# Low half of a weight pair by one VectorE subtraction in place of a cast and an adding DMA, with a newly planned order, in a chain of attention and two expert layers

## The chip, the cores and the metric

The kernel runs on one core of a Trainium2 chip. The metric is the time of one execution in microseconds (us) on the device, the median over several runs. Inputs and outputs lie in HBM.

## The reference

The reference chains three blocks on 1536 rows of 512 numbers (float32). Local attention with a window of 16 keys on each side, plus 24 block summaries for each head, gives `x`. Then come two layers of dense experts, 4 experts in the first and 8 in the second:

```
for e in range(E):                      # E = 4, then 8
    h = np.maximum(x @ w1[e], 0.0)      # 512 -> 1024
    out += p[:, e:e + 1] * (h @ w2[e])  # 1024 -> 512
```

In the first layer `p` are the given shares of each row, divided by their sum. In the second, `p` comes from a gate, `x @ w_gate`, and eight rounds in which rows and columns are normalised in turn.

## The kernel before

**Units and steps.** A unit is one expert's slice of 256 hidden columns: 16 units in the first layer, 32 in the second, so 48 in all. A step is one unit on one of the two halves of 768 rows (`b` = 0 or 1), so there are 96 steps. Each step has a first part (`add_first`, tensors `w1`, matmuls at L294) and a second part (`add_second`, tensors `w2`, matmuls at L593). The second part of a step runs interleaved with the first part of the next step.

**Seven products.** Both parts multiply 2 x 2 blocks by a scheme of seven products instead of eight, so weights and rows enter as blocks and as sums of blocks. The operands of the weights are named A11, A12, A22, S1, S2, S3 and S4, where the S are sums. The orders in which a step does its products are written out by hand as strings (`FIRST`, `SECOND`), in which digit 5 is the product with S1, 6 the one with S2, 3 with S4 and 7 with S3.

**High and low halves.** Every operand is held as two float32r tensors, a rounded high half and a low half that holds the rest. A product is three matmuls of 128 x 384 in a row: high by high, high by low, low by high. The tiles are `w1hi`, `w1lo`, `w2hi`, `w2lo` for weights, `xhi`, `xlo`, `x11..` for the rows of the first part and `hoph` for both halves of the rows of the second.

**Weights** (`add_weights`). SyncE loads the four blocks of a slice into a raw buffer (three of these turn: `raw1`, `raw2` and `xf`). ScalarE casts three blocks to the high half (L471) and writes the same blocks, negated and rounded, to the low half (L472); GpSimd then starts a DMA that adds the raw blocks to the low half (L475), so that the rest stays there. Then three adding DMAs in place (L482) make the sums in the raw buffer. Then the pair S1, S2 and the pair S4, S3 get the same treatment as the blocks: cast, negated write, adding DMA, each 128 x 512. Blocks A12, A22, A11 have two sets of slots that alternate by unit. The four sums have only one set, so the cast of a new pair waits until TensorE has read the old pair for the last time.

**Row operands.** `add_hop` prepares the operands of the second part: ScalarE writes the high half (L453), VectorE the low half by one subtraction (`lo_op`, L448 or L443). Results are added up by VectorE (L229) or by ScalarE copies through PSUM (L604).

**Who sets the order.** All work is collected with `op(engine, span, reads, writes, due, ...)` and put in order by `run_work`, a planner that runs when the program is built. It knows a time for each kind of work (`SPAN`; for DMAs four numbers: issue, start-up, time on the shared DMA engines, landing), takes the work that can start first by those times, and breaks ties by `due`, which is counted in steps. The instructions then stand in each engine's queue in that order, and each queue is executed in order. `LEAD` and `LEAD2` say how many steps ahead weights and their pairs are due, `HOP` and `DCOFF` when the operands and the second half of the columns of the second part are due, `ALONG`, `FIRST0`, `XDUE`, `W0DUE`, `XPOOL` place the attention, the first step, the row operands and the first weights, `TURN`, `LATER` and `SOONER` place work around the border between the layers (`add_turn`, `add_scale`).

Of the kernel before, what the change touches and what calls it, by code (L numbers as in the profile page):

```python
# [18 lines left out]
def local_global_attention_moe_moe(  # L19
# [287 lines left out]
    def relu(S, out, src, th, neg=False):  # L307
# [9 lines left out]

    ADD = 0.72  # L320
    SPAN = {
# [5 lines left out]
        "v1536": (1.3, 1.34), "vmax": (0.57, 0.65), "vsum": (0.57, 0.66), "vrec": (0.12, 0.18),  # L327
        "vks": (0.6, 0.69), "vks2": (0.35, 0.42), "vkw": (0.7, 0.81), "vq": (1.0, 1.1),
        "vvb": (0.22, 0.3), "vmk": (0.82, 0.83), "vid": (1.1, 1.15),
        "a": (0.41, 0.48), "ah": (0.42, 0.52), "a512": (0.53, 0.63), "a768": (0.74, 0.84),  # L330
        "as": (0.2, 0.26), "akw": (0.8, 0.91), "aq": (0.95, 1.04), "aexp": (1.05, 1.12),
        "ax": (0.31, 0.38),
        "p256": (0.75, 0.77), "p384": (1.05, 1.08), "psm": (0.98, 1.02), "pks": (0.8, 0.85),
        "pid": (0.55, 0.6), "p1": (0.2, 0.25), "pmask": (3.0, 3.1), "psel": (0.9, 0.95),
        "add1": (0.87, 1.2, ADD, 1.2), "add2": (0.87, 1.2, 2 * ADD, 1.2),
        "add3": (0.87, 1.2, 3 * ADD, 1.2), "ld": (0.45, 1.0, 0.6, 1.8), "st": (0.45, 0.5, 0.5, 1.2),
        "ldk": (0.45, 1.0, 0.8, 1.2), "ldv": (0.45, 1.0, 1.3, 1.2), "lds": (1.4, 1.6, 1.2, 1.2),
        "ldp": (0.45, 1.0, 0.5, 1.2),
    }
    HOP_WAIT = 0.09  # L340
    work = []
    last_write, last_reads = {}, {}

# [92 lines left out]
    def aop(fn, reads, writes, due, span="a", use=None):  # L436
        op("ACT", span, reads, writes, due, fn, use=use)
# [17 lines left out]
    def add_weights(u, kind, start):  # L455
        hi, lo = wop[kind]
        i = turn_of(kind, u)
        R = [("raw", i, j) for j in range(4)]
        for o, x, blocks in loads(kind, u):
            first = XF if (kind, u) == (1, 2) else []  # L460
            op(
                "SP", "ld", [("mark", WAIT0)] if u == 0 else (),
                [R[j] for j in blocks] + first, start,
                lambda o=o, x=x: nc.sync.dma_start(out=o, in_=x),
            )

        def group(s, src, blocks, key, due, span):
            n = len(blocks)
            h, l = hi[:, s:s + n], lo[:, s:s + n]
            rd = [R[j] for j in blocks]  # L470
            aop(lambda: nc.scalar.copy(out=h, in_=src), rd, [key + ("hi",)], due, span)  # L471
            aop(lambda: nc.scalar.mul(l, src, -1.0), rd, [key + ("lo",)], due, span)  # L472
            op(
                "POOL", f"add{n}", rd, [key + ("lo",)], due + 0.05,
                lambda: nc.gpsimd.dma_start(out=l, in_=src, accum_op=ALU.add),  # L475
            )

        group(slot(u, A12), raws[i][:, 0:3], (0, 1, 2), wkey(kind, u, A12), start + 0.2, "a768")
        for o, x, wr, rd in sums_of(kind, u):
            op(  # L480
                "POOL", f"add{len(wr)}", [R[j] for j in (*rd, *wr)], [R[j] for j in wr], start + 0.5,
                lambda o=o, x=x: nc.gpsimd.dma_start(out=o, in_=x, accum_op=ALU.add),  # L482
            )
        group(6, *pair_of(kind, u, 0), wkey(kind, u, S1), start + LEAD2, "a512")
        group(8, *pair_of(kind, u, 1), wkey(kind, u, S4), start + LEAD2 + 0.1, "a512")

    def wk(kind, u, x):
        k = wkey(kind, u, x)
        return [k + ("hi",), k + ("lo",)]
# [505 lines left out]
    def add_loads(i, d):  # L995
        b, hp = pairs[i]
        for j in range(2):
            op(
                "SP", "ldk", (), [("kn", j)] + ([("mark", i)] if j else []), d,
                lambda j=j: nc.sync.dma_start(  # L1000
                    out=kn[:, :, j, :], in_=k[b, 2 * hp + j].rearrange("(c p) d -> p c d", p=P)
                ),
            )
        for j in range(2):
            op(
                "SP", "ldk", (), [("qn", j)], d + 0.01,
                lambda j=j: nc.sync.dma_start(
                    out=qn[:, j],
                    in_=q[b, 2 * hp + j].rearrange("(c p r) d -> p c (r d)", p=P, r=2),
                ),  # L1010
            )
        op(
            "SP", "ldv", (), ["vn"], d + 0.3,
            lambda: nc.sync.dma_start(
                out=vn, in_=v[b, 2 * hp:2 * hp + 2].rearrange("h (p c) d -> p h c d", c=VC)
            ),
        )
        t = vs[i % 2]

        def windows(j):  # L1020
            src = v[b, 2 * hp + j]
            mid = bass.AP(
                src.tensor, src.offset + (QT - WIN) * D, [[D, KW], [QT * D, NQ - 2], [1, D]]
            )
            nc.sync.dma_start(out=t[0:KW, 0, j, :], in_=src[0:KW, :])
            nc.sync.dma_start(out=t[0:KW, 1:NQ - 1, j, :], in_=mid)
            nc.sync.dma_start(out=t[0:KW, NQ - 1, j, :], in_=src[S - KW:S, :])

        for j in range(2):
            op("SP", "lds", (), [("vs", i % 2, j)], d + 0.35, lambda j=j: windows(j))  # L1030

    def add_keys(i, d):
# [50 lines left out]
        def spread():  # L1083
# [4 lines left out]
                )  # L1088

        op(  # L1090
            "POOL" if KSPOOL else "DVE", "pks" if KSPOOL else "vks",
            [("ks", p, 0), ("ks", p, 1)], [("kw", p, 2)], d + 0.03, spread,
        )

# [152 lines left out]
    def add_rows_first(d):  # L1247
        op(
            "SP", "ldp", [("mark", 1)], ["dp"], d,
            lambda: nc.sync.dma_start(out=dp, in_=domain_probs.rearrange("(t p) e -> p t e", p=P)),  # L1250
        )
        op(
            "SP", "ldp", [("mark", 1)], ["wg"], d,
            lambda: nc.sync.dma_start(out=wg, in_=w_gate.rearrange("(c p) e -> p c e", p=P)),
        )

        def shares():
            nc.vector.tensor_reduce(out=dsum, in_=dp, axis=AX.X, op=ALU.add)
            nc.vector.tensor_scalar_add(out=dsum, in0=dsum, scalar1=1e-9)
            nc.vector.reciprocal(out=dsum, in_=dsum)  # L1260
            nc.vector.tensor_tensor(
                out=p1.rearrange("x e t -> x t e"), in0=dp,
                in1=dsum[:, :, None].to_broadcast([P, NTT, E1]), op=ALU.mult,
            )

        vop(shares, ["dp"], ["p1"], d, "v768", True)
        tk = take_of(0)
        n = E1 * NTT
        op(
            "PE", "tr", ["p1", "ident"], ["prt"], d,  # L1270
            lambda: nc.tensor.transpose(
                full[tk["bank"]][0:n, 0:P], p1.rearrange("x e t -> x (e t)"), ident
            ),
            take=tk,
        )
        aop(
            lambda: nc.scalar.copy(out=rowt[0:n], in_=full[tk["bank"]][0:n, 0:P]),
            ["prt"], ["rowt"], d, "as", use=tk,
        )
        op("SP", "st", ["rowt"], ["prow1"], d, lambda: save_rows(0))  # L1280

        def halves():
            nc.scalar.copy(out=wghl[:, :, 0:E2], in_=wg)

        def lows():
            nc.vector.tensor_tensor(
                out=wghl[:, :, E2:2 * E2], in0=wg, in1=wghl[:, :, 0:E2].bitcast(F32),
                op=ALU.subtract,
            )
            nc.vector.tensor_tensor(  # L1290
                out=fold, in0=ident[0:2 * E2, 0:E2], in1=ident[0:2 * E2, E2:2 * E2], op=ALU.add
            )

        aop(halves, ["wg"], ["wghi"], d + 4.0, "as")
        vop(lows, ["wghi", "ident"], ["wghl"], d + 4.0, "vs", True)

    def set_places():

# [18 lines left out]
    L = E1 * NFU - 1  # L1317
    steps = [(u, b, 2 * u + b) for u in range(NU) for b in range(2)]
    border = 2 * L + 1
    FIRST = {0: "1567324", 1: "1562374"}  # L1320
    SECOND = {0: "1256437", 1: "1524637"}
    HOP, GOFF, DCOFF, LEAD, LEAD2 = 1.15, 0.16, 3.9, 1.0, 0.97
    LOPOOL = ()
    ALONG = 8.8
    NARROW = 4
    WAIT0 = 2
    KSPOOL = False
    XDUE = [-5.4, -2.8, -2.0, 0.3]
    W0DUE = -3.0
    FIRST0 = -1.1  # L1330
    XPOOL = [(B22, T3), (N1, B21, T3, N4), (T3, N4), (B22, N4)]
    LATER = {1: -0.4, 2: -0.4, 3: 0.6, 8: -0.4}
    SOONER = {0: 0.4, 2: -0.4, 3: -0.4, 6: 0.2, 7: 0.2}
    TURN = 0.8
    M2ACT = True
    with tc.manual_schedule():
        ps = ctx.enter_context(tc.tile_pool(name="ps", bufs=1, space=PSUM))
        full = [ps.tile([P, 512], F32, name=f"bank{i}") for i in range(8)]
# [33 lines left out]
        op("SP", "ld", ["prow1"], [("pb", 1)], -0.5, lambda: load_row(PB[1], 0, 0, 1))  # L1372
        for j, key in enumerate(("pz", ("bank", 3), ("bank", 4), ("bank", 5), ("bank", 6))):
            op(
                "PE", "one", [("x", 0, 0, B11)] + wk(1, 0, A11), [key], 0.1,
                lambda j=j: nc.tensor.matmul(
                    cut[2 + j], wop[1][0][:, SLOT[A11], 0:P], x_of(0, 0, 0, B11),
                    start=True, stop=True, skip_group_check=True,
                ),
            )  # L1380
# [65 lines left out]
```

## Time and profile before

| | |
|---|---|
| median of 3 runs | 1564.73 us (1563.39 to 1567.13) |
| profiled execution, own time | 1563.7 us |
| span from first to last instruction | 1562.0 us |
| TensorE (PE) busy | 1522.5 us, 97% |
| weight loads (PEld) busy | 1489.1 us, 95% |
| VectorE (DVE) busy | 1303.5 us, 83% |
| ScalarE (ACT) busy | 1201.3 us, 77% |
| GpSimd (POOL) busy | 608.7 us, 39% |
| granted TensorE clock, mean | 0.997 of 2.4 GHz |
| DMA started by GpSimd | 151.03 MB, 60.6% of the 16 DMA engines |

The times of engines are unions of their instructions' times, and overlap. A matmul that follows another closely starts before the other's record ends. The profiled execution took 1.0 us less than the median.

### The profile page before, as it was taken

How to read it: one execution, taken by the hardware profiler on the slowest of the kernel's cores; microseconds unless marked ns; L12 is line 12 of the kernel's file. 1: busy time of each engine (PE TensorE's matmuls, PEld its weight loads, DVE VectorE, ACT ScalarE, POOL GpSimd, SP SyncE). 2: the span in 40 equal slices, each digit the busy share in tenths (PEclk: the TensorE clock that was granted, in tenths of full speed). 3: DMA queues.
4: the chain of work that ended last, by engine and by line, in shares of the span. 5: the costliest groups of instructions: out<-in, count | busy, mean ns of one | idle time of the engine just before them, and what ended most of it. 6: DMA issues, size and time to landing. Idle time of an engine off the chain costs nothing.

```text
span 1562.0 us, 26666 instructions
## 1 busy us (share of the span) xinstructions
PE 1522.5 (97%) x9106; PEld 1489.1 (95%) x9106; DVE 1303.5 (83%) x2717; ACT 1201.3 (77%) x2587; POOL 608.7 (39%) x632
## 2 busy tenths in 40 slices
PE   8899999999999999999999999999999999999998
PEld 7799999999999988999999999999999999999997
DVE  7787788788888897899888888888888887888888
ACT  6798688687777779777777778777877877868865
POOL 3553434434343332333343343443434343443430
PEclk9999999999999999999999999999999999999999
DMA  9978888878778874697878778878878887888863
GB/s 213 219 152 148 149 154 149 150 146 153 147 149 149 149 130 94 120 182 133 149 142 156 149 139 161 153 139 155 146 139 159 149 145 150 150 149 150 151 108 95
DMA packets 223865, 231.13 MB, mean 148 GB/s; under 512 B 48736, under 2 KB 169968, under 8 KB 223728
## 3 DMA queue, kind: packets, MB, share of 16 engines
q0 software_dynamic: 107520, 151.03, 60.6%
q1 hardware_dynamic: 116208, 78.39, 17.9%
q8 instruction: 71, 1.16, 0.3%
q14 instruction: 66, 0.54, 0.1%
HBM read 73.97 MB, written 3.22 MB: 49 GB/s over the span
## 4 chain that ended last, share of the span: by engine, by line
PE 72%; DMA 14%; DVE 5%; issue 4%; ACT 3%; POOL 2%; SPq 0%; POOLq 0%; ACTq 0%; DVEq 0%
PE bank L294 34%; PE bank L593 33%; DMA w2lo<-raw 4%; DMA w1lo<-raw 2%; DMA w2lo<-xf 2%; DMA w1lo<-xf 2%; DMA raw<-raw 2%; DVE acc L229 1%; PE bank L1168 1%; DMA vn<-in_v_dram 1%; PE bank L1132 1%; PE bank L1229 1%; ACT hoph L453 1%; PE bank L1214 1%; DVE hoph L448 1%
## 5 line engine op out<-in xcount | busy, mean ns | idle before, releaser
L593 PE MATMUL bank<-hoph,w2hi 128*128 128x384 f32 x2688 | 687.9, 336 | 9.0 <-ACT bank L604 6.1
L593 PEld LDWEIGHTS bank<-hoph,w2hi 128*128 128x128 f32 x2688 | 483.1, 188 | 14.8 <-ACT bank L604 8.3
L593 PE MATMUL bank<-hoph,w2lo 128*128 128x384 f32 x1344 | 451.8, 336 | 8.7 <-DMA w2lo<-raw 6.0
L229 DVE TENSOR_TENSOR acc<-bank,acc 128x384 f32<-128x384 f32 x736 | 392.5, 551 | 7.0 <-PE bank L593 5.0
L294 PE MATMUL bank<-xhi,w1hi 128*128 128x384 f32 x1008 | 339.7, 337 | 1.8 <-ACT xhi L453 1.1
L294 PE MATMUL bank<-xlo,w1hi 128*128 128x384 f32 x1008 | 337.8, 335 | 0.4 <-DVE xlo L443 0.4
L294 PE MATMUL bank<-xhi,w1lo 128*128 128x384 f32 x1008 | 337.6, 335 | 0.2 <-DMA w1lo<-xf 0.2
L482 POOL DMA_DIRECT2D raw<-raw x195 | 194.7, 1000 | 304.3 <-DMA raw<-raw 182.6
L604 ACT COPY bank<-bank 128x384 f32<-128x384 f32 x384 | 181.1, 472 | 153.8 <-PE bank L593 146.8
L453 ACT ACTIVATE hoph<-q 128x384 fp32r<-128x384 f32 x576 | 288.6, 519 | 7.7 <-PE bank L593 4.3
L448 DVE TENSOR_TENSOR hoph<-q,hoph 128x384 fp32r<-128x384 f32 x486 | 259.7, 549 | 27.1 <-ACT hoph L453 26.9
L593 PEld LDWEIGHTS bank<-hoph,w2lo 128*128 128x128 f32 x1344 | 252.2, 188 | 15.2 <-DMA w2lo<-raw 10.6
L294 PEld LDWEIGHTS bank<-xhi,w1hi 128*128 128x128 f32 x1008 | 189.5, 188 | 5.4 <-ACT xhi L453 1.4
L294 PEld LDWEIGHTS bank<-xlo,w1hi 128*128 128x128 f32 x1008 | 189.6, 188 | 0.7 <-DVE xlo L443 0.7
L294 PEld LDWEIGHTS bank<-xhi,w1lo 128*128 128x128 f32 x1008 | 189.5, 188 | 0.5 <-DMA w1lo<-xf 0.5
L475 POOL DMA_DIRECT2D w1lo<-raw x96 | 95.3, 993 | 173.8 <-ACT w1lo L472 136.1
L482 POOL DMA_DIRECT2D xf<-xf x93 | 92.3, 992 | 166.1 <-DMA xf<-xf 101.0
L604 ACT COPY acc<-bank 128x384 f32<-128x384 f32 x220 | 105.0, 479 | 56.3 <-PE bank L593 46.6
L475 POOL DMA_DIRECT2D w2lo<-raw x99 | 108.5, 1098 | 93.4 <-ACT w2lo L472 53.5
L604 ACT COPY bank<-acc 128x384 f32<-128x384 f32 x176 | 85.1, 483 | 55.3 <-DVE acc L229 51.5
L311 DVE SCALAR_TENSOR_TENSOR q<-bank,pb 128x384 f32<-128x384 f32 x180 | 99.5, 553 | 23.2 <-PE bank L294 18.9
L232 DVE TENSOR_TENSOR q<-q,bank 128x384 f32<-128x384 f32 x96 | 53.1, 553 | 71.0 <-PE bank L294 68.1
(180 smaller groups left out, 2168.3 us busy)
## 6 DMA issues: line engine op xcount, KB each, us to landing
raw<-raw POOLq DMA_DIRECT2D x130, 256.0 KB, 3.8
raw<-in_moe_w_dram SPq DMA_DIRECT2D x66, 256.0 KB, 5.0
w2lo<-raw POOLq DMA_DIRECT2D x66, 256.0 KB, 4.1
raw<-in_moe_w_dram SPq DMA_DIRECT2D x128, 128.0 KB, 3.3
w1lo<-raw POOLq DMA_DIRECT2D x64, 256.0 KB, 4.0
xf<-xf POOLq DMA_DIRECT2D x62, 256.0 KB, 3.8
w2lo<-raw POOLq DMA_DIRECT2D x33, 384.0 KB, 5.4
w1lo<-raw POOLq DMA_DIRECT2D x32, 384.0 KB, 5.7
```

Of the source, the lines that this page charges most:

```text
L229: (eng or nc.vector).tensor_tensor(out=out, in0=x, in1=y, op=ALU.add)
L232: (eng or nc.vector).tensor_tensor(out=out, in0=x, in1=y, op=ALU.subtract)
L294: nc.tensor.matmul(pm, l[:, s, cs_], x_of(b, c, r, x), start=first and i == 0, stop=i == n - 1, skip_group_check=True,)
L311: nc.vector.scalar_tensor_tensor(out=out, in0=src, scalar=0.0, in1=PB[S[1]][:, th * HB:(th + 1) * HB], op0=ALU.min if neg else ALU.max, op ...
L448: e.tensor_tensor(out=out, in0=src, in1=hi.bitcast(F32), op=ALU.subtract)
L453: aop(lambda: nc.scalar.mul(to(0), src, -1.0 if neg else 1.0), reads, writes, due, "ah")
L475: lambda: nc.gpsimd.dma_start(out=l, in_=src, accum_op=ALU.add),
L482: lambda o=o, x=x: nc.gpsimd.dma_start(out=o, in_=x, accum_op=ALU.add),
L593: nc.tensor.matmul(cut[bank], l[:, s, cols], hop_of(t, r), start=start and i == 0, stop=i == 2, skip_group_check=True,)
L604: aop(lambda: nc.scalar.copy(out=out, in_=src), [kin], [kout], due)
L1132: nc.tensor.matmul(pv[KW:KX, 0:P], sel[:, c, :], vn[:, :, c, :], start=c == 0, stop=c == VC - 1,)
L1168: nc.tensor.matmul(pw[:, tt * KX:(tt + 1) * KX], bd[p][:, g * GT + tt].rearrange("x j q -> x (j q)"), kw[p][(g * GT + tt) // KT][:, (g * G ...
```

## The change

In `add_weights` the function `group` gets a switch. For the pairs named in `LODVE`, which is the pair S1, S2 of both `w1` and `w2`, the low half is made by one VectorE subtraction, raw minus high half, as `lo_op` does it for rows. ScalarE's negated write and GpSimd's adding DMA of that pair fall away. The pair S4, S3 and the three blocks stay as they were. The planner's times of DMAs and a few names of spans are new, and its constants are new, so the order of all work is planned anew.

```diff
-    ADD = 0.72
+    ADD = 1.0
...
-        "add1": (0.87, 1.2, ADD, 1.2), "add2": (0.87, 1.2, 2 * ADD, 1.2),
-        "add3": (0.87, 1.2, 3 * ADD, 1.2), "ld": (0.45, 1.0, 0.6, 1.8), "st": (0.45, 0.5, 0.5, 1.2),
-        "ldk": (0.45, 1.0, 0.8, 1.2), "ldv": (0.45, 1.0, 1.3, 1.2), "lds": (1.4, 1.6, 1.2, 1.2),
-        "ldp": (0.45, 1.0, 0.5, 1.2),
+        "add1": (0.95, 1.3, ADD, 1.2), "add2": (0.950001, 1.3, 2 * ADD, 1.2),
+        "add3": (0.950002, 1.3, 3 * ADD, 1.2), "ld": (0.45, 1.0, 0.65, 1.3),
+        "st": (0.450001, 0.5, 0.5, 1.2), "ldk": (0.450002, 1.0, 1.2, 1.2),
+        "ldq": (0.450003, 1.0, 0.6, 1.2), "ldv": (0.450004, 1.0, 1.0, 1.2),
+        "lds": (1.4, 1.6, 1.8, 1.2), "ldp": (0.450005, 1.0, 0.6, 1.2),
...
-    HOP_WAIT = 0.09
+    HOP_WAIT = 0.08
...
-        def group(s, src, blocks, key, due, span):
+        def group(s, src, blocks, key, due, span, by_dve=False):
             n = len(blocks)
             h, l = hi[:, s:s + n], lo[:, s:s + n]
             rd = [R[j] for j in blocks]
             aop(lambda: nc.scalar.copy(out=h, in_=src), rd, [key + ("hi",)], due, span)
+            if by_dve:
+                vop(
+                    lambda: vsub(l, src, h.bitcast(F32)), rd + [key + ("hi",)],
+                    [key + ("lo",)], due + 0.05, "v512",
+                )
+                return
             aop(lambda: nc.scalar.mul(l, src, -1.0), rd, [key + ("lo",)], due, span)
...
-        group(6, *pair_of(kind, u, 0), wkey(kind, u, S1), start + LEAD2, "a512")
-        group(8, *pair_of(kind, u, 1), wkey(kind, u, S4), start + LEAD2 + 0.1, "a512")
+        for i, s in enumerate((S1, S4)):
+            group(
+                SLOT[s], *pair_of(kind, u, i), wkey(kind, u, s), start + LEAD2 + i / 10, "a512",
+                (kind, s) in LODVE,
+            )
...
-    FIRST = {0: "1567324", 1: "1562374"}
+    FIRST = {0: "5162374", 1: "1562374"}
     SECOND = {0: "1256437", 1: "1524637"}
-    HOP, GOFF, DCOFF, LEAD, LEAD2 = 1.15, 0.16, 3.9, 1.0, 0.97
+    HOP, GOFF, DCOFF, LEAD, LEAD2 = 1.18, 0.16, 3.1, 1.93, 0.99
     LOPOOL = ()
-    ALONG = 8.8
+    ALONG = 8.2
...
-    XDUE = [-5.4, -2.8, -2.0, 0.3]
-    W0DUE = -3.0
-    FIRST0 = -1.1
-    XPOOL = [(B22, T3), (N1, B21, T3, N4), (T3, N4), (B22, N4)]
-    LATER = {1: -0.4, 2: -0.4, 3: 0.6, 8: -0.4}
-    SOONER = {0: 0.4, 2: -0.4, 3: -0.4, 6: 0.2, 7: 0.2}
-    TURN = 0.8
+    XDUE = [-4.5, -1.5, -2.4, 1.2]
+    W0DUE = -0.7
+    FIRST0 = 0.9
+    XPOOL = [(N1, B21, B22, T3, N4), (N1, B22, T3, N4), (T3, N4), (B11, N1, B21, B22, N4)]
+    LATER = {-2: 1.0, 0: 0.4, 1: -0.4, 3: 1.0, 6: -0.2, 8: -0.4}
+    SOONER = {-1: -0.2, 1: 0.8, 2: 0.4, 3: 0.2, 6: 1.0, 7: 0.2, 8: 1.0}
+    TURN = 1.0
     M2ACT = True
+    LODVE = ((1, S1), (2, S1),)
```

## Rows read from the trace of the kernel before

**Rows 1.** Busy time by stage: stretch, length, then engines with their instructions.

```profile
0.00:110.00 110.00, 96.80 (x963) 85.36 (x964) 87.20 (x202) 85.05 (x231) 50.79 (x69) 0.98 0.95 201
110.00:560.00 450.00, 445.54 (x2544) 441.03 (x2544) 368.70 (x744) 350.87 (x744) 182.23 (x184) 1.00 0.80 147
560.00:720.00 160.00, 152.50 (x856) 142.25 (x856) 142.26 (x348) 126.63 (x275) 55.13 (x56) 0.99 0.72 136
720.00:1530.00 810.00, 802.90 (x4598) 797.83 (x4597) 679.34 (x1373) 624.57 (x1314) 319.81 (x324) 1.00 0.79 145
```

**Rows 2.** TensorE's waits, 110 to 560 us: total, times, longest.

```profile
PE bank L593 <- DMA w2lo<-raw: 2.3, 6, 0.7
PE bank L593 <- ACT bank L604: 2.0, 3, 1.0
```

**Rows 3.** TensorE's waits, 720 to 1530 us.

```profile
PE bank L593 <- DMA w2lo<-raw: 3.7, 7, 1.2
PE bank L593 <- DMA w2lo<-xf: 2.4, 4, 0.8
PE bank L593 <- ACT bank L604: 0.7, 1, 0.7
```

**Rows 4.** The chain that ended last, in order of time: start, length, what.

```profile
196.15 2.09 PE bank L294 x12
...
551.98 2.09 PE bank L294 x12
...
567.42 1.90 DVE acc L229 x4
...
754.73 2.09 PE bank L294 x12
...
1230.19 2.09 PE bank L294 x12
...
1259.36 2.09 PE bank L294 x12
...
1495.76 2.09 PE bank L294 x12
```

**Rows 5.** Timeline around one wait: start, length, engine, line; idle before and releaser.

```profile
1079.52 0.90 POOL L482 DMA_DIRECT2D raw<-raw  x1 [1.53 <-DMA raw<-raw]
1079.61 0.55 DVE L448 TENSOR_TENSOR hoph<-q,hoph 128x384 fp32r<-128x384 f32 x1
...
1080.95 0.61 ACT L471 CAST w2hi<-raw 128x512 fp32r<-128x512 f32 x1
...
1081.47 0.63 ACT L472 ACTIVATE w2lo<-raw 128x512 fp32r<-128x512 f32 x1
...
1082.53 1.20 POOL L482 DMA_DIRECT2D raw<-raw  x1 [2.11 <-DMA raw<-raw]
1082.54 0.56 DVE L448 TENSOR_TENSOR hoph<-t,hoph 128x384 fp32r<-128x384 f32 x1 [0.85 <-ACT hoph L453]
...
1083.25 1.41 POOL L475 DMA_DIRECT2D w2lo<-raw  x1
...
1085.08 1.20 POOL L475 DMA_DIRECT2D w2lo<-raw  x1 [0.42 <-ACT w2lo L472]
```

**Rows 6.** Timeline of TensorE at the same place.

```profile
1088.00 0.44 PE L593 MATMUL bank<-hoph,w2lo 128*128 128x384 f32 x1 [1.19 <-DMA w2lo<-raw]
```

**Rows 7.** Groups of instructions: count, busy us, mean ns, idle before.

```profile
L448 DVE TENSOR_TENSOR hoph<-q,hoph 128x384 fp32r<-128x384 f32 x486 | 259.7, 549 | 27.1 <-ACT hoph L453 26.9
L908 DVE COPY xf<-bank 128x512 f32<-128x512 f32 x4 | 2.7, 682 | 0.3 <-DMA out_dram<-xf 0.3
L593 PE MATMUL bank<-hoph,w2hi 128*128 128x384 f32 x2688 | 687.9, 336 | 9.0 <-ACT bank L604 6.1
```

**Rows 8.** DMA issues: count, KB each, median us from issue to landing.

```profile
w2lo<-raw POOLq DMA_DIRECT2D x66, 256.0 KB, 4.1
```

**Rows 9.** Busy time in 10 us stretches around the border between layers, columns as in Rows 1.

```profile
570.00:580.00 10.00, 8.24 (x37) 6.24 (x35) 10.00 (x22) 5.47 (x12) 3.81 (x5) 0.83 0.87 169
...
690.00:700.00 10.00, 7.11 (x38) 6.15 (x37) 10.00 (x23) 6.65 (x15) 5.95 (x6) 1.00 0.91 165
```

**Rows 10.** The chain that ended last at 592 us.

```profile
592.34 0.62 ACT w2lo L472
```

**Rows 11.** TensorE's waits, 0 to 110 us.

```profile
PE bank L1132 <- DMA vn<-in_v_dram: 6.0, 3, 2.8
```

**Rows 12.** The chain that ended last, around one late copy of ScalarE's.

```profile
883.55 5.03 DMA raw<-in_moe_w_dram
```

More of the change, by code (lines that the diff above doesn't have):

```diff
@@ L327, in local_global_attention_moe_moe @@
         "v1536": (1.3, 1.34), "vmax": (0.57, 0.65), "vsum": (0.57, 0.66), "vrec": (0.12, 0.18),
-        "vks": (0.6, 0.69), "vks2": (0.35, 0.42), "vkw": (0.7, 0.81), "vq": (1.0, 1.1),
-        "vvb": (0.22, 0.3), "vmk": (0.82, 0.83), "vid": (1.1, 1.15),
+        "vks": (0.6, 0.69), "vksw": (0.600001, 0.69), "vks2": (0.35, 0.42), "vkw": (0.7, 0.81), "vq": (1.0, 1.1),
+        "vvb": (0.22, 0.3), "vsh": (0.870001, 0.97), "vlow": (0.150001, 0.2), "dum": (0.110002, 0.3), "vmk": (0.82, 0.83), "vid": (1.1, 1.15),
         "a": (0.41, 0.48), "ah": (0.42, 0.52), "a512": (0.53, 0.63), "a768": (0.74, 0.84),
@@ L1005, in add_loads @@
             op(
-                "SP", "ldk", (), [("qn", j)], d + 0.01,
+                "SP", "ldq", (), [("qn", j)], d + 0.01,
                 lambda j=j: nc.sync.dma_start(
@@ L1090, in add_keys @@
         op(
-            "POOL" if KSPOOL else "DVE", "pks" if KSPOOL else "vks",
+            "POOL" if KSPOOL else "DVE", "pks" if KSPOOL else "vksw",
             [("ks", p, 0), ("ks", p, 1)], [("kw", p, 2)], d + 0.03, spread,
@@ L1264, in shares @@
             )
-        vop(shares, ["dp"], ["p1"], d, "v768", True)
+        vop(shares, ["dp"], ["p1"], d, "vsh", True)
         tk = take_of(0)
@@ L1294, in add_rows_first @@
         aop(halves, ["wg"], ["wghi"], d + 4.0, "as")
-        vop(lows, ["wghi", "ident"], ["wghl"], d + 4.0, "vs", True)
+        vop(lows, ["wghi", "ident"], ["wghl"], d + 4.0, "vlow", True)
     def set_places():
@@ L1374, in local_global_attention_moe_moe @@
             op(
-                "PE", "one", [("x", 0, 0, B11)] + wk(1, 0, A11), [key], 0.1,
+                "PE", "dum", [("x", 0, 0, B11)] + wk(1, 0, A11), [key], 0.1,
                 lambda j=j: nc.tensor.matmul(
```

## Prediction

> **What bounds the kernel now.** I read the stages first [rows 1]. TensorE is busy 445.5 of 450 us in the first layer's steady stretch and 802.9 of 810 us in the second's, so the matmuls set the time, and only what interrupts them can be won there. The attention (110 us, 13 us idle) and the border between the layers (160 us, 7.5 us idle) are the loose places.
>
> Busy time hides part of a stall, since a matmul's record of 336 ns [rows 7] overlaps the next one. So I read the pace from the chain in order of time, where one place of the order comes back once a unit [rows 4]. An undisturbed unit takes 1259.36 - 1230.19 = 29.17 us; twelve matmuls take 2.09 us, 0.174 us each. From 196.15 to 551.98 lie 12 units: 355.83 us, 5.8 more than 12 x 29.17. From 754.73 to 1495.76 lie 25 units: 741.03 us, 11.8 more. The steady stretches thus lose 17.6 us in 37 units.
>
> TensorE's waits say to what [rows 2, 3]. For the low half of `w2` it idles 2.3 + 3.7 + 2.4 = 8.4 us in 17 waits. Each also loses what the overlap hides, 0.336 - 0.174 = 0.16 us, so they cost 8.4 + 17 x 0.16 = 11.2 us. Four waits for a copy of ScalarE cost 2.7 + 4 x 0.16 = 3.3 us. Together that is 14.5 us, most of the excess.
>
> One of these waits in the timeline [rows 5, 6]: ScalarE finishes the high half of the pair S1, S2 at 1081.56 us and the negated write at 1082.10. GpSimd's queue has an adding DMA for `raw` in front, which waits 2.11 us for an earlier landing, so the pair's DMA is issued only at 1083.25. TensorE gets its low half at 1088.00, 4.75 us later, after 1.19 us of idling; the pair S4, S3, issued at 1085.08, is not waited for. By its place in GpSimd's queue the first pair is what is late in all these waits but the two earliest, which are the second pair's.
>
> **The change part by part.**
>
> *Low half of the first pair.* At 1081.56 VectorE could subtract. A subtraction of 128x384 takes 549 ns; a 128x512 operation takes 682 [rows 7], and that is my duration. Back to back, VectorE starts one of 128x384 every 0.47 us (four in 1.90) [rows 4], so one of 512 columns holds it for 0.47 + 0.13 = 0.60 us. The low half would be there at about 1082.3, 5.6 us before it came by DMA [rows 5, 6]. The largest wait is 1.2 us [rows 3], so these should all go. The later pair also stands nearer the front of both queues. I take the full 11.2 us; the bounds are 0 (if another wait takes the place) and 11.2.
>
> *Work on VectorE.* 96 subtractions (two kinds, 48 units) of 0.60 us are 58 us. In the second layer's stretch VectorE is idle 810.0 - 679.3 = 130.7 us in 27.7 units, 4.7 us a unit [rows 1], against 1.2 us added. In the place shown it idles 0.85 us at just that time [rows 5]. Covered, so nothing. Around the border there is no cover: VectorE is busy 10.00 of 10 us at 570 and at 690 [rows 9]. Four subtractions at most belong to the units there, 2.4 us; I take half, +1.2 us.
>
> *Work taken from ScalarE.* 96 negated writes of 0.63 us [rows 5]. At 592 us such a write lies on the chain with 0.62 us [rows 10]: -0.5 us, bounds 0 and -1.2 (two of them). The four late copies [rows 2, 3] stand in ScalarE's queue behind casts that wait for a load or a sum, such as the load of 883.55 us that took 5.03 us [rows 12]. A queue with 96 fewer writes, and loads due earlier (`LEAD` 1.0 to 1.93), should free half: -1.7 us, bounds 0 and -3.3.
>
> *Work taken from GpSimd and the DMA engines.* 96 issues of about 1.2 us [rows 5] and 96 x 256 KB = 25 MB, which take 4.1 us each to land [rows 8]. This costs nothing and gives nothing by itself; the raw blocks of the pair are free earlier, since a subtraction read them and not a DMA.
>
> *New planning.* A unit's loads (4 for `w1`, 2 for `w2`), its casts, six remaining adding DMAs of GpSimd and the subtractions get earlier due times. They go past hop operations in ScalarE's and VectorE's queues and past row loads (`pb`) in SyncE's. Due times only break ties, so each can put an operation before another that was equally ready, for about one instruction's length (0.5 to 0.6 us), against the 4.7 us of slack; a blocked head of SyncE's queue would hold the loads behind it. The planner's adding DMA of 256 KB now lasts 1.3 + 2.0 + 1.2 = 4.5 us where it had 3.84, and rows say 4.1 [rows 8]: the old plan was too hopeful, the new one errs on the safe side. `DCOFF` 3.9 to 3.1 brings the second half of the columns nearer to the first, with the same four PSUM banks. I set all of this at nothing in the steady stretches.
>
> *Attention and first step.* TensorE waits 6.0 us there for `vn` loads [rows 11]. Loads, row operands, first weights (`W0DUE` -3.0 to -0.7) and first products (`FIRST0` -1.1 to 0.9) all get new places, and two adding DMAs fall away while the DMA engines are 0.95 busy [rows 1]. I can't say which way this goes: 0, bounds -6 (no wait for `vn`) and +6 (as many new ones).
>
> A rule to weigh against this: a GpSimd issue of 0.90 us ran while VectorE subtracted with two SBUF inputs at 1079.61 [rows 5], no slower than the 1.20 and 1.41 us of others. The Trainium skill, "SBUF — State Buffer", section "Who interferes with whom", says that a VectorE instruction with two SBUF inputs contends with a GpSimd instruction that reads SBUF, and not with one that only writes. The trace agrees for issues. By that rule GpSimd's multiplications of the attention could each be held for one subtraction, 0.68 us; with the two of unit 0 the sum would be 1.4 us longer. I leave this out.
>
> The sum: -11.2 + 1.2 - 0.5 - 1.7 = -12.2 us against the profiled execution's own 1563.7 us (its span is 1562.0), so 1551.5 us. That execution was 1.0 us under the median of the runs, so I predict **1552 us** for the median.
>
> **The rivals.**
>
> *More than that.* The better times in the plan also remove the rest of the excess (17.6 - 12.9 = 4.7 us) and the waits for `vn` (6.0). For it speaks that the plan was wrong about exactly the DMAs that are late. Against it: the rest is spread over many small gaps with no common releaser. 1552 - 10.7 = 1541 us.
>
> *The wait moves.* The plan, which takes S1 for early now (`FIRST` begins with 5 for `w1`), may use all four sums sooner, and the pair S4, S3 still comes by DMA. It is issued at 1085.08 [rows 5]; with 4.1 to 4.75 us to land it is there at 1089.2 to 1089.8, only 1.2 to 1.8 us after the first pair. If its products stand that much earlier, TensorE waits as before: 1552 + 11.2 = 1563 us, no change. The two waits of the second pair early in the run speak for it; against it, that this pair loses a queue neighbour on ScalarE and on GpSimd, about 0.5 and 1.2 us.
>
> *VectorE frees the banks late.* VectorE also adds results out of PSUM (L229). Its queue is in order, and each subtraction waits for a cast on ScalarE, which may itself wait for a sum's landing; the additions behind it wait too, and with `DCOFF` 3.1 TensorE wants the banks sooner. Between 720 and 1530 us no wait of TensorE's for VectorE stands among its waits, which speaks against it; VectorE's 84% there [rows 1] speaks for it. It decides once each of the 96 subtractions costs TensorE more than 12.2 / 96 = 0.13 us. At a third of its 0.60 us the kernel gets 19 us: 1552 + 19 = 1571 us, slower.
>
> *The first unit comes late.* With `W0DUE` 2.3 steps later the first weights are loaded later, and products that now fill gaps of the attention stand behind it. At most the idle of the attention opens again, 13 us [rows 1]: 1552 + 13 = 1565 us, the same time as before.
>
> **How the numbers follow.** Chances: the forecast 0.62 (its own range 1546 to 1559, from the bounds of border, copies and attention), more than that 0.14, the wait moves 0.09, banks late 0.09, first unit late 0.06. A measurement here tells about 0.2% (3 us) from no change. Faster than 1561.6: 0.62 + 0.14, and 0.05 of the moved wait and the late first unit, where only part of the gain is lost: 0.81. The same: 0.09. Slower: 0.10, nearly all of it from the banks. The range that leaves out 2 in 10 reaches from 1542, nearly the best case, to 1565, the case of a late first unit.
>
> **What would show it.** Right: ScalarE's 128x512 negated writes halved (192 to 96), 96 VectorE subtractions of 128x512 at about 0.68 us, GpSimd's queue at 126 MB; the waits of L593 for `w2lo` gone or under 1 us in sum; units at 29.2 us nearly throughout; VectorE at about 88%. Wrong: waits of L593 or L294 for VectorE (L229, L448) or for ScalarE's copies in the steady stretches; waits for `w2lo` that stay, then of the second pair; or an attention stage that ends later than 110 us.

## Result and profile after

The changed kernel takes 1552.04 us, the median of four runs (1550.06 to 1554.43), against 1564.72 us before: 0.9918 of it, with a 95% interval of 0.9897 to 0.9939. That is 0.8% faster, and the forecast was 1552. The profiled execution of after is the slowest of its four, 1554.43 us (span 1552.7); against 1563.7 it shows 9.3 of the 12.7 us that separate the medians.

The stages of after, with the columns of [rows 1]:

```profile
0.00:110.00 110.00, 94.96 (x932) 82.94 (x932) 83.69 (x192) 80.56 (x218) 51.32 (x69) 0.95 0.90 187
110.00:560.00 450.00, 449.34 (x2590) 447.01 (x2590) 393.89 (x787) 343.25 (x727) 161.32 (x159) 1.00 0.72 134
560.00:720.00 160.00, 153.10 (x829) 141.50 (x828) 142.97 (x347) 119.89 (x255) 45.49 (x45) 0.96 0.59 114
720.00:1520.00 800.00, 799.97 (x4607) 799.40 (x4606) 717.96 (x1432) 595.38 (x1261) 272.18 (x268) 1.00 0.69 129
```

In the second layer TensorE now idles 0.03 us in 800. Its waits there, a list of several lines in [rows 3], are empty. In the first layer there are two, where [rows 2] had nine in two lines:

```profile
PE bank L603 <- ACT bank L614: 0.5, 1, 0.5
PE bank L603 <- DVE hoph L449: 0.2, 1, 0.2
```

(L603, L614 and L449 are before's L593, L604 and L448.) The chain in time, which answers to [rows 4], has the pace. The first two rows are 6 units apart, the last two 23:

```profile
316.26 2.09 PE bank L294 x12
491.26 2.09 PE bank L294 x12
...
815.93 2.09 PE bank L294 x12
...
1486.76 2.09 PE bank L294 x12
```

175.00 / 6 and 670.83 / 23 are both 29.17 us, the undisturbed unit. The groups of the new subtractions, then two groups of transfers (DMA view: count, size, median us from issue to landing), the halved ones of the low half and those of the raw sums:

```profile
L232 DVE TENSOR_TENSOR w2lo<-raw,w2hi 128x512 fp32r<-128x512 f32 x33 | 22.8, 690 | 1.4 <-ACT w2hi L472 0.7
L232 DVE TENSOR_TENSOR w1lo<-raw,w1hi 128x512 fp32r<-128x512 f32 x32 | 21.8, 681 | 2.3 <-ACT w1hi L472 2.1
```

```profile
w2lo<-raw POOLq DMA_DIRECT2D x33, 256.0 KB, 4.4
raw<-raw POOLq DMA_DIRECT2D x130, 256.0 KB, 4.8
```

The place of the order that [rows 5, 6] showed, in the timeline of after:

```profile
1079.13 0.60 ACT L472 CAST w2hi<-raw 128x512 fp32r<-128x512 f32 x1
...
1079.77 0.69 DVE L232 TENSOR_TENSOR w2lo<-raw,w2hi 128x512 fp32r<-128x512 f32 x1
```

The low half stands at 1080.46, 0.7 us after its cast ended; before, it came 6.4 us after.

Where the time went is read from the units' starts, taken by counting the 128x384 matmuls of the two parts in the trace (168 a unit), in the profiled executions (us):

| stretch | before | after | difference |
|---|---|---|---|
| start to unit 1 | 128.68 | 133.08 | +4.4 |
| units 1 to 15 | 416.86 | 410.12 | -6.7 |
| border, units 15 to 20 | 173.45 | 178.30 | +4.9 |
| units 20 to 47 | 799.54 | 788.03 | -11.5 |
| the end | | | -0.3 |

The steady stretches gave 18.2 us where 12.9 was forecast; the border took 4.9 more where 0.7 was forecast, and the start 4.4 more where 0 was. TensorE's granted clock is 1.00 in both kernels' steady stretches (the stages above and [rows 1]), so the clock has no part in the 18.2 us.

### The profile page after: what moved, and what is told of

Same layout as the page of the kernel before. It is cut to its first block, busy times and chain, and to the rows that moved or that the text cites. A ratio compares the mean times of both kernels' runs of the same rounds, so it can differ in the third digit from the quotient of the medians.

```text
span 1552.7 us, 26796 instructions
## 1 busy us (share of the span) xinstructions
PE 1522.8 (98%) x9106; PEld 1494.5 (96%) x9106; DVE 1365.4 (88%) x2807; ACT 1154.2 (74%) x2491; POOL 531.5 (34%) x542
## 3 DMA queue, kind: packets, MB, share of 16 engines
q1 hardware_dynamic: 116208, 78.39, 18.2%
## 4 chain that ended last, share of the span: by engine, by line
PE 89%; DVE 5%; ACT 4%; DMA 1%; issue 1%; POOL 0%; SPq 0%; DVEq 0%; ACTq 0%; POOLq 0%
PE bank L294 43%; PE bank L603 42%; DVE acc L229 1%; ACT s L1200 1%; PE bank L1142 1%; DVE q L232 1%; PE bank L781 1%; PE bank L1178 1%; PE bank L1239 1%; DVE q L311 0%; DVE acc L235 0%; PE bank L1224 0%; DVE hoph L449 0%; ACT acc L614 0%; ACT hoph L454 0%
## 5 line engine op out<-in xcount | busy, mean ns | idle before, releaser
L603 PE MATMUL bank<-hoph,w2hi 128*128 128x384 f32 x2688 | 688.4, 336 | 4.5 <-ACT bank L614 2.9
L603 PEld LDWEIGHTS bank<-hoph,w2hi 128*128 128x128 f32 x2688 | 484.5, 188 | 10.7 <-ACT bank L614 6.0
L603 PE MATMUL bank<-hoph,w2lo 128*128 128x384 f32 x1344 | 449.6, 335 | 0.0
L229 DVE TENSOR_TENSOR acc<-bank,acc 128x384 f32<-128x384 f32 x736 | 393.5, 552 | 30.3 <-PE bank L603 29.5
L454 ACT ACTIVATE hoph<-q 128x384 fp32r<-128x384 f32 x576 | 296.9, 522 | 69.8 <-DVE q L311 49.8
L489 POOL DMA_DIRECT2D raw<-raw x195 | 226.6, 1162 | 242.4 <-DMA raw<-raw 100.1
L449 DVE TENSOR_TENSOR hoph<-q,hoph 128x384 fp32r<-128x384 f32 x486 | 255.3, 550 | 15.9 <-ACT hoph L454 10.9
L603 PEld LDWEIGHTS bank<-hoph,w2lo 128*128 128x128 f32 x1344 | 252.7, 188 | 0.0
L614 ACT COPY bank<-bank 128x384 f32<-128x384 f32 x384 | 181.1, 472 | 46.0 <-PE bank L603 37.3
L489 POOL DMA_DIRECT2D xf<-xf x93 | 107.5, 1156 | 124.1 <-DMA xf<-xf 58.1
L614 ACT COPY acc<-bank 128x384 f32<-128x384 f32 x220 | 104.5, 476 | 55.5 <-PE bank L603 54.1
L614 ACT COPY bank<-acc 128x384 f32<-128x384 f32 x176 | 84.6, 480 | 78.0 <-DVE acc L229 77.9
L482 POOL DMA_DIRECT2D w1lo<-raw x64 | 67.7, 1058 | 214.5 <-ACT w1lo L479 204.8
L482 POOL DMA_DIRECT2D w2lo<-raw x66 | 68.4, 1036 | 168.7 <-ACT w2lo L479 155.4
L472 ACT CAST w1hi<-raw 128x512 fp32r<-128x512 f32 (+1 forms) x96 | 65.7, 689 | 58.6 <-PE bank L294 57.7
```

The lines of the kernel that those rows point to most:

```text
L229: (eng or nc.vector).tensor_tensor(out=out, in0=x, in1=y, op=ALU.add)
L449: e.tensor_tensor(out=out, in0=src, in1=hi.bitcast(F32), op=ALU.subtract)
L454: aop(lambda: nc.scalar.mul(to(0), src, -1.0 if neg else 1.0), reads, writes, due, "ah")
L603: nc.tensor.matmul(cut[bank], l[:, s, cols], hop_of(t, r), start=start and i == 0, stop=i == 2, skip_group_check=True,)
L614: aop(lambda: nc.scalar.copy(out=out, in_=src), [kin], [kout], due)
```

## Experiments

Each time is the median of 4 to 10 runs; ratios are to the kernel before on the same chip, with 95% intervals. What is said of units, waits and the clock is read from one profiled execution of each kernel. In the expectations, one side holds the shorter path of the low halves responsible for the gain, the other the plan: the times and constants from which the order is made. The first seven take the change apart, the next four price the subtraction, and the last does it for one kind of weight alone.

**1. The new plan without the subtraction** (against after):

```diff
-    LODVE = ((1, S1), (2, S1),)
+    LODVE = ()
```

> The changed kernel with LODVE empty: new DMA times and constants in the plan, but the low half of the first pair by cast and adding DMA as before. Theory P (the path of that low half was too long): the waits of the second part for w2lo come back with 8 to 11 us in sum, units of 29.5 to 30.5 us, time 1560 to 1566 us. Rival Q (the truer DMA times of the plan made the gain, the subtraction is incidental): waits for w2lo stay under 2 us, units at 29.2 us, time 1550 to 1555 us.

1655.27 us, 1.0573 (1.0550 to 1.0596): far worse than either side's numbers, and by another wait. TensorE's waits between 300 and 540 us:

```profile
PE bank L603 <- DVE acc L229: 9.1, 14, 0.7
```

Nothing waits for `w2lo` there. The banks turn on VectorE's additions, some two waits a unit, and a unit takes 31.6 us; these waits do not cover all of the 2.4 us lost a unit. The loss stands in the plan already: by the start times that the planner gives the work while the program is built, a unit between 20 and 47 takes 31.7 us in this kernel (measured: 31.5) and 29.13 in after (measured: 29.19). One reason can be added up from the new rows of `SPAN`: the adding DMAs of a unit move 24 blocks and six loads go with them, so the plan puts 24 x 1.0 + 6 x 0.65 = 27.9 us of transfers on the shared DMA engines in a unit of 29.17. With the subtraction it is 23.9, and by the old times 20.9 without it. So this run shows what the planner makes of the long path, and not what the path itself would cost on the chip.

**2. The old planned times and constants with the subtraction** (against before):

```diff
+            if by_dve:
+                vop(lambda: vsub(l, src, h.bitcast(F32)), ...)
+                return
...
+    LODVE = ((1, S1), (2, S1),)
```

> The kernel before with nothing but the subtraction for the first pair of w1 and w2: old DMA times and old constants, order planned with the subtraction in it. Theory P: w2lo waits gone, steady units mostly at 29.2 us, 1564.7 - 11 to 17 = 1548 to 1554 us, and attention and border as before, so perhaps below the changed kernel. Rival Q: the plan is as wrong as before about the other DMAs, some other transfer is late, 1560 to 1566 us.

1575.44 us, 1.0067 (1.0044 to 1.0089): the path alone makes the kernel slower, by more than either side said. The `w2lo` waits do go (one of 0.9 us is left), so the mechanism is there, but TensorE and ScalarE wait for something else. TensorE's waits from 720 to 1530 us, then ScalarE's for DMAs there:

```profile
PE bank L602 <- ACT bank L613: 9.6, 15, 1.6
PE bank L602 <- DMA w2lo<-raw: 0.9, 1, 0.9
```

```profile
ACT w1hi L471 <- DMA raw<-in_moe_w_dram: 11.7, 7, 2.9
ACT w1hi L471 <- DMA raw<-raw: 8.3, 6, 1.8
ACT w1hi L471 <- DMA xf<-xf: 3.9, 3, 1.4
ACT w1hi L471 <- DMA xf<-in_moe_w_dram: 3.8, 3, 1.7
```

ScalarE stands 27.7 us at the head of its queue with a cast whose load or sum has not landed; before it was 4.7 us, in after 0.8. One such place in its timeline:

```profile
835.25 0.84 ACT L471 CAST w1hi<-raw 128x768 fp32r<-128x768 f32 x1 [1.51 <-DMA raw<-in_moe_w_dram]
835.99 0.47 ACT L613 COPY bank<-bank 128x384 f32<-128x384 f32 x1
836.40 0.52 ACT L453 ACTIVATE hoph<-q 128x384 fp32r<-128x384 f32 x1
836.51 0.30 PEld L602 LDWEIGHTS bank<-hoph,w2hi 128*128 128x128 f32 x2 [0.80 <-ACT bank L613]
836.51 0.61 PE L602 MATMUL bank<-hoph,w2hi 128*128 128x384 f32 x2 [0.48 <-ACT bank L613]
```

The cast waits 1.51 us for a load, the copy that frees a bank stands behind it, and TensorE behind the copy. Here the loss is not planned: the planner has 29.12 us a unit between 20 and 47, the trace 29.78.

By stages the run looks better than its total. Units 1 to 15 take 412.14 us, 4.7 less than before, and units 20 to 47 take 804.17, 4.6 more, so the steady stretches come out even. The 11 us lost lie before unit 1 (+3.4) and in the border (+7.6).

**3. The old kernel with only the new planned times** (against before):

```diff
-    ADD = 0.72
+    ADD = 1.0
...
-    HOP_WAIT = 0.09
+    HOP_WAIT = 0.08
```

with all the other rows of `SPAN` as in the change; no subtraction, old constants.

> The kernel before with nothing but the new times of DMAs in the plan (and the hop wait of 0.08): no subtraction, old constants. Theory P: the path stays as long as it was, w2lo waits of 8 to 11 us stay, 1560 to 1567 us. Rival Q: waits for w2lo fall under 3 us, 1553 to 1557 us.

1633.21 us, 1.0432 (1.0411 to 1.0453). TensorE's waits, the first two of the whole span:

```profile
PE bank L594 <- DVE acc L229: 14.2, 24, 1.0
PE bank L294 <- DVE q L232: 11.1, 11, 1.0
```

As in the first, the order is planned slower, 30.9 us a unit between 20 and 47 (measured: 30.8), and again VectorE's work stands in the list. Longer planned times win nothing by themselves.

**4. Subtraction and new times, old constants** (against after: `FIRST`, `HOP` to `LEAD2`, `ALONG`, `XDUE` to `TURN`, and three names of spans as before).

> The kernel before with the subtraction and the new DMA times in the plan, all constants old. The subtraction alone left 28 us of ScalarE waiting for loads and sums at the head of its queue (19 waits between 720 and 1530 us) and TensorE behind its copies. Theory S (the plan's DMA times put the casts before their data): with the new times these waits fall under 3 us, steady units at 29.2 us, 1550 to 1558 us. Rival C (it is the constants, above all weights due 0.93 step sooner): ScalarE's waits for DMAs stay over 10 us and the time at 1568 to 1578 us.

1569.43 us, 1.0029 (1.0017 to 1.0041). ScalarE's waits for DMAs from 720 to 1520 us shrink from 27.7 to

```profile
ACT w1hi L472 <- DMA raw<-raw: 1.3, 3, 0.6
```

That much is as the plan's side has it: the times keep ScalarE's queue from standing. Most steady units take 29.17 to 29.5 us, and the steady stretches are 10.0 us shorter than before. The total is still above the kernel before, since unit 1 starts at 134.59 us and the border takes 182.6.

**5. Subtraction and new constants, old times** (against after):

```diff
-    ADD = 1.0
+    ADD = 0.72
...
-    HOP_WAIT = 0.08
+    HOP_WAIT = 0.09
```

> The changed kernel with the old DMA times and hop wait in the plan: subtraction and all new constants. Theory S: ScalarE waits 10 us or more for DMAs at the head of its queue, TensorE behind it, 1562 to 1575 us. Rival C: these waits stay under 3 us and steady units at 29.2 us, 1550 to 1556 us.

1582.32 us, 1.0097 (1.0067 to 1.0127). ScalarE waits 11.6 us for DMAs in that stretch, and TensorE for ScalarE:

```profile
PE bank L602 <- ACT acc L613: 3.5, 7, 0.9
```

**6. Subtraction and the constants of the steady units, old times** (against before: the subtraction, and the new `FIRST` and `HOP, GOFF, DCOFF, LEAD, LEAD2`).

> The kernel before with the subtraction and only five new constants and one order of the steady stretch (HOP, GOFF, DCOFF, LEAD, LEAD2, FIRST); old DMA times, old constants of attention and border. Theory S: as the run before, ScalarE's waits for DMAs stay over 10 us, 1562 to 1578 us. Rival C: waits under 3 us, steady units at 29.2 us, 1548 to 1555 us.

1573.97 us, 1.0057 (1.0034 to 1.0081); ScalarE waits 8.7 us for DMAs. Loads due earlier (`LEAD` 1.93) don't stand in for truer times.

**7. All but the constants of the edges** (against after):

```diff
-    ALONG = 8.2
+    ALONG = 8.8
...
-    W0DUE = -0.7
-    FIRST0 = 0.9
+    W0DUE = -3.0
+    FIRST0 = -1.1
```

and `XDUE`, `XPOOL`, `LATER`, `SOONER` and `TURN` as before too.

> The changed kernel with the old constants of the attention, the first step and the border (ALONG, XDUE, W0DUE, FIRST0, XPOOL, LATER, SOONER, TURN). The changed kernel reached its first full unit 4.4 us later and crossed the border 4.9 us more slowly than the kernel before. If the new constants of these stages cost that: first unit at about 129 us, border 5 us shorter, 1541 to 1547 us. Rival: the old constants were fitted to the old order and fit the new one worse, then first unit later than 133 us or a longer border, 1553 to 1570 us; steady units at 29.2 us either way.

1562.32 us, 0.9977 (0.9964 to 0.9990). Nearly every steady unit takes 29.17 us, so subtraction, times and steady constants make the steady gain. Unit 1 starts at 136.46 us and the border takes 183.51, 3.4 and 5.2 us more than in after: the old edge constants do not suit the new order.

The ratios as a staircase, each step with one more part; then, from the units' starts, the difference from before in us in the steady stretches (units 1 to 15 and 20 to 47) and at the edges (up to unit 1, and the border):

| kernel | ratio | steady | edges |
|---|---|---|---|
| before | 1 | 0 | 0 |
| subtraction alone | 1.0067 | -0.1 | +10.9 |
| and new times | 1.0029 | -10.0 | +15.1 |
| and constants of the steady units | 0.9977 | -19.1 | +17.8 |
| and constants of the edges (the change) | 0.9918 | -18.2 | +9.3 |
| the change without its subtraction | 1.0573 | +80.4 | +12.4 |

The totals hide this: the steady gain grows from step to step, while every new order here loses time at the edges, where half clock comes in too (experiment 9).

**8. Each subtraction twice, in after's order**:

```diff
-                    lambda: vsub(l, src, h.bitcast(F32)), rd + [key + ("hi",)],
+                    lambda: [vsub(l, src, h.bitcast(F32)) for _ in range(2)], rd + [key + ("hi",)],
```

> The changed kernel with each of the 96 subtractions done twice, in the same order of all work: 96 x 0.60 us = 58 us more on VectorE. Theory P with the slack of VectorE counted from the trace (about 3 us a unit left): steady units stay at 29.2 us, only the border, where VectorE is busy throughout, gets 1 to 2.5 us longer: 1552 to 1555 us. Rival V (VectorE is the next bound, banks come free late): units lengthen by 0.3 us or more, 1563 us and over.

1569.09 us, 1.0019 (1.0008 to 1.0030). The chain in time, one unit from row to row:

```profile
1001.25 2.09 PE bank L294 x12
1030.72 2.09 PE bank L294 x12
1060.18 2.09 PE bank L294 x12
1089.62 2.09 PE bank L294 x12
```

A unit takes 29.46 us, 0.29 to 0.30 more, for two more subtractions: 0.15 us each on average. Yet VectorE idled 800 - 717.96 = 82 us of after's 800, 3.0 us a unit. The two need less than half of it: in the trace the second of a pair starts 0.73 us after the first, so they hold VectorE for 1.46 us a unit. Idle time is not all to be had. A pair in the timeline, and the first line of what TensorE's weight loads wait for from 720 to 1520 us:

```profile
1002.59 1.42 DVE L232 TENSOR_TENSOR w2lo<-raw,w2hi 128x512 fp32r<-128x512 f32 x2
```

```profile
PEld bank L603 <- DVE acc L229: 5.3, 28, 0.6
```

That is one wait a unit for a bank that VectorE frees, the mechanism of the rival "VectorE frees the banks late". In after this line is not there. In the unit shown the starts of TensorE's matmuls lie apart by more than usual in one place alone, from 1006.0 to 1008.9 us, after the pair of `w2`.

**9. The border's subtractions shrunk**: after's order, with the ten from `w2` of unit 15 to `w1` of unit 20 on 2 of 256 columns of each block.

```diff
-                    lambda: vsub(l, src, h.bitcast(F32)), rd + [key + ("hi",)],
+                    lambda: (vsub(l[:, :, 0:2], src[:, :, 0:2], h[:, :, 0:2].bitcast(F32)) if 31 < 2 * u + kind < 42 else vsub(l, src, h.bitcast(F32))), rd + [key + ("hi",)],
```

> The changed kernel in its own order, but the 10 subtractions of the units at the border between the layers (w2 of unit 15 to w1 of unit 20) work on 2 of 256 columns of each block, so the rest of these low halves is left out. Theory B (VectorE's added work is what lengthened the border): doubling lengthened it by 2.6 us, so nearly as much comes off, 1549 to 1550 us against 1552 for the full one, border 175.5 us against 178.3. If all of the 4.9 us came from the subtractions, 173 us. Rival (the border is longer because its order is another and TensorE's granted clock falls in it): 0 to 1 us.

1549.78 us, 0.9895 (0.9877 to 0.9913). The interval overlaps with that of after, so the gain is read from the border in the traces: it takes 176.27 us, 2.0 less. TensorE's granted clock differs there. Windows of after, and of this kernel at the same place:

```profile
568.00:571.00 3.00, 1.59 (x6) 0.94 (x6) 3.00 (x8) 1.71 (x5) 0.31 (x1) 0.97 1.09 228
571.00:574.00 3.00, 2.73 (x7) 1.63 (x8) 3.00 (x7) 1.51 (x4) 0.90 (x1) 0.50 0.68 111
574.00:578.00 4.00, 4.00 (x15) 3.54 (x15) 4.00 (x10) 2.03 (x4) 0.86 (x1) 0.50 0.33 51
578.00:582.00 4.00, 4.00 (x17) 4.00 (x16) 3.11 (x7) 1.73 (x5) 1.20 (x1) 0.62 0.45 66
```

```profile
568.00:571.00 3.00, 1.91 (x6) 1.14 (x6) 3.00 (x7) 1.98 (x4) 0.90 (x1) 0.66 0.69 109
571.00:574.00 3.00, 3.00 (x17) 2.37 (x15) 3.00 (x8) 1.51 (x3) 0.86 (x1) 0.77 0.48 83
574.00:578.00 4.00, 3.18 (x16) 2.60 (x16) 4.00 (x9) 1.69 (x5) 1.20 (x1) 1.00 0.28 41
```

After a stretch in which TensorE worked 1.59 of 3 us, its clock in after is at 0.50 (1.2 GHz) until about 581; here it is back at full by 574. In all, 10.2 us at half against 3.4. At half clock a matmul of 128x384 follows the last every 0.32 us instead of 0.174, so a stretch loses up to 46% of its length, and 6.8 us of it are worth up to 3.1 us: the clock can account for the whole 2.0. The profiled execution of after also has the lowest mean clock of its four (0.992; the others 0.995 and 0.996), so part of the 2.0 may be that execution's alone.

Experiment 8 tells more. Its border has half clock twice for 3.4 us, as this one has, and takes 180.87 us. So at equal clock the ten subtractions done twice cost 4.6 us against the ten left out (five units at the steady 0.30 us would be 1.5): their time on VectorE does count at the border. And more work on VectorE did not bring the longer half clock. What the single subtraction costs there stays open.

The clock bears on the whole loss of the border. [rows 9] had a granted clock of 0.83 and 1.00 in these two places; after has 0.54 and 0.86:

```profile
570.00:580.00 10.00, 8.96 (x29) 7.17 (x28) 10.00 (x23) 4.17 (x9) 2.95 (x3) 0.54 0.45 73
690.00:700.00 10.00, 7.58 (x35) 6.75 (x34) 9.66 (x22) 4.27 (x8) 4.77 (x5) 0.86 0.82 143
```

Over the border that is 13.6 us at half clock in after against 3.4 before. The 10.2 us more are worth up to 4.7 of the 4.9 us.

**10. All subtractions but unit 0's shrunk**, in after's order: the same edit with `if u > 0`.

> The same for the 94 subtractions of all units but the first: VectorE does 55 us less, the order of all work stays, the low halves of the first pair are left out for the most part. Theory (in the steady stretches the single subtraction is covered): units stay at 29.17 us, and only what e9 shows comes off, 1548 to 1551 us. Rival V (VectorE sets the pace already, as the doubled subtractions, 0.15 us each, suggest): units under 29.1 us, 1540 to 1546 us.

1546.91 us, 0.9876 (0.9858 to 0.9893). The windows of the second layer's stretch:

```profile
720.00:1520.00 800.00, 799.97 (x4607) 799.40 (x4606) 690.65 (x1429) 594.56 (x1260) 271.25 (x267) 1.00 0.68 129
```

TensorE's 799.97 us and the unit's 29.17 are those of after, though VectorE has 27 us less to do. In the steady stretch a single subtraction costs nothing. The border takes 176.28, as in the kernel with only the border's shrunk. The time is under the 1548 us expected at least, and no run of this kernel is as slow as the fastest of experiment 9. In the traces the difference lies before unit 1 (3.3 us) and in one unit (0.8 us), and why is open.

**11. The border's subtractions on GpSimd**, planned at 1.4 us there, the rest planned anew around them (against after):

```diff
+            if by_dve and 31 < 2 * u + kind < 42:
+                op(
+                    "POOL", "p512", rd + [key + ("hi",)], [key + ("lo",)], due + 0.05,
+                    lambda: vsub(l, src, h.bitcast(F32), nc.gpsimd), True,
+                )
+                return
...
```

> The changed kernel with the 10 subtractions of the border done by GpSimd in place of VectorE (planned with 1.4 us each), all work done. If VectorE's load lengthens the border by 0.25 us a subtraction: 2 to 3 us faster than the changed kernel, 1548 to 1551 us. Rival (GpSimd takes longer and the order is planned anew): the border gets longer, 1553 to 1562 us.

1554.25 us, 0.9922 (0.9903 to 0.9941): not to be told from after. The border takes 181.05 us and the half clock lasts 10.2 us again, from 567.1. This attempt to win the 2 us back with all the work done fails.

**12. Subtraction for `w2` alone** (against after):

```diff
-    LODVE = ((1, S1), (2, S1),)
+    LODVE = ((2, S1),)
```

> The changed kernel with the subtraction for w2 alone; w1's first pair gets its low half by cast and adding DMA. TensorE hardly ever waited for w1lo in the kernel before (0.2 us). Theory P: only the low half of w2 was late, so w1's part brings nothing: steady units at 29.2 us, 1550 to 1556 us. Rival (w1's adding DMA stands in GpSimd's queue and its negated write in ScalarE's, in front of w2's work, and the plan has to make room): units of 29.4 us or more, 1562 to 1600 us.

1583.88 us, 1.0114 (1.0093 to 1.0136). For a low half of `w1` TensorE waited only once in the steady stretches before, 0.2 us, yet without its subtraction the new plan loses 2%. Steady units take 29.2 to 31.5 us, and the waits are again for VectorE's L229 and ScalarE's L614. As in experiments 1 and 3 the loss is planned: 30.0 us a unit between 20 and 47, measured 29.8. So within this plan not only `w2`'s path matters; that a late low half of `w1` would hold up TensorE on the chip is not shown.

## Why the prediction was right, and where it was not

**Low half of the first pair, -11.2: its waits go, the price is not confirmed.** They are gone in after, and experiment 2 shows that the subtraction does that by itself. What didn't follow is that the time comes with it: alone it gives 0.1 us in the steady stretches, and +0.7% in all.

**New planning, set at nothing: the step that failed.** "Due times only break ties" took the order as a detail. With the subtraction in place, new times and steady constants bring the steady stretches from -0.1 us to -19.1; that is the gain. Without the subtraction the new times and constants make the kernel 5.7% slower, the new times alone 4.3%, and both losses stand in the plan already. With the subtraction, the old times let ScalarE's casts stand for loads that land later than planned. The sentence that the old plan was "too hopeful" was right, but it was used as harmless, not as the condition of the gain. That the new one "errs on the safe side" has a price too, which the shorter path lowers: 27.9 us of planned transfers a unit without it, 23.9 with it.

**Late copies, -1.7: mis-sized.** Their idling went from 2.7 us to 0.5, and the rest of the excess went too: of 17.6 us over 29.17 a unit nothing is left between the rows of the chain shown, against 12.9 forecast. For this the change needed the new times, not the 96 fewer writes, since experiment 2 has the fewer writes and 27.7 us of waiting on ScalarE.

**VectorE, "covered": right by luck.** One subtraction a kind and unit costs nothing (experiment 10), but a second costs 0.15 us of its 0.73 (experiment 8). The working took 4.7 us of idle time a unit as room for 1.2; the room ends somewhere between 1.2 and 2.7 us. The rival of banks freed late did not happen in after; experiment 8 shows it with one more subtraction a kind, and waits for L229 stand in the plans without the full subtraction.

**Border, +1.2 and -0.5: mis-sized.** It measured +4.9. Between units 15 and 20 lie not four subtractions but ten, and with them shrunk 2.0 us go, clock included. The other 2.8 us stay, with 6.8 us at half clock against 3.4 before, worth up to 1.6 of them. The sum had no term for TensorE's clock, which could make up nearly all of the 4.9. By the planner's own times the border takes 172.4 us in after and 170.3 before, so some of it may be the order's; how the two share it was not taken apart. The -0.5 for ScalarE isn't confirmed.

**Attention, 0 with bounds of 6: within them.** The wait for `vn` [rows 11] fell from 6.0 to 1.1 us, yet unit 1 starts 4.4 us later in the profiled execution. Kernels with after's order there started unit 1 at 127.58, 130.87, 131.98 and 133.08 us (experiments 10, 9, 8 and after), around before's 128.68. Experiment 11, with after's order up to the border and the same work there, starts it at 128.13. TensorE's half clock goes with this: experiment 11 has none before unit 1, after has 10.2 us, experiment 9, with the same work too, 3.4. So no loss by the order is established, and this scatter is large enough to make the 2.4 us by which the profiled execution lies above its median.

That the total hit is luck, since errors cancel: 5.3 us too little gain in the steady stretches, 4.2 us too little loss at the border. Of the rivals, "more than that" happened in the steady stretches, and "the wait moves" not at all. Open is which of the new times, the longer landing or the larger share of the DMA engines, makes the plans without the full subtraction slow. Open is also how much any change of the planner's inputs would cost: the old edge constants suit the new order badly (experiment 7), and no run changes the order for a reason that has nothing to do with this change. No version run here beats the changed kernel with all its work done.

## What to carry to other kernels

A shorter path and the planner's knowledge of it belong together: here each alone cost 0.7 to 5.7%, both won 0.8%, and constants fitted to one order cost time in the next. Where an order is planned, compare the planned DMA times and the planned pace with the traced ones first: here the plans without the full subtraction were slow as planned, the one with the old times only on the chip. Look for queue heads that wait, since the delay passes on to whatever stands behind, as in experiment 2. Split a total by stages before judging a part by it. Measure the room on a busy engine by doubling the added work, not by its idle time.

## What the runs showed of the hardware

VectorE, 90% busy in the steady stretch (717.96 of 800 us), took 0.73 us more work every half unit only at 0.15 us of TensorE's time (experiment 8). Two subtractions of 128x512 into the same tile start 0.73 us apart; before another operation the subtraction holds VectorE for 0.60. After a pause of TensorE's in the border, the half clock lasted 10.2 us in after and 3.4 in three kernels with its order whose subtractions are shrunk or doubled (experiments 8, 9 and 10); matmuls of 128x384 then follow each other every 0.32 us instead of 0.174. The raw sums' adding DMAs of 256 KB took longer in after (4.8 us against 3.8), though 96 of the adding DMAs are gone.
